# Attention with a threshold, then SoLU and a layer norm, in one kernel: the copy of o ahead of V on ScalarE, the last tokens' product mixed in later, loads of q, k and v in other rounds, and the last tile's h a tile sooner

## The chip, the cores and the metric

The kernel runs on one core of a Trainium2 chip. The metric is the device time of one execution in microseconds (us). Names used here: TensorE (PE in the profile, its weight loads PEld), VectorE (DVE), ScalarE (ACT), GpSimd (POOL), and SyncE (SP), whose queue issues nearly all DMAs. Each of these takes its own instructions in the order in which the program lists them.

## The reference

Eight batches of eight heads, 576 tokens, 64 numbers a head; then 4608 tokens of width 512 through a layer of width 1024 and back, all in float32.

```python
scores = (1/sqrt(64)) * q @ k.T
scores = where(scores >= max(scores) - tau, scores, -1e9)
attn   = exp(scores - max) / (sum + 1e-9)
x      = heads side by side of attn @ v            # 4608 x 512
h      = x @ w_in                                  # 4608 x 1024
solu   = h * softmax(h)
ln     = (solu - mean) / sqrt(var + 1e-6) * g_ln
out    = ln @ w_out                                # 4608 x 512
```

## The kernel before

The program is laid out in rounds, by hand (`manual_schedule`): the loop at the end of the kernel counts `rnd` and lists, for each engine, what this round adds. There are 144 rounds with scores (NS), 18 to a batch (PER), and then a tail without scores. A batch starts at round 18 b, so batches of even number start at a round that divides by 4, and those of odd number at one that leaves 2.

**Attention.** Each round makes the scores of one slot (`scores`, L479): two heads, 128 rows of queries, 576 keys. VectorE takes the row limit (`maxes`, L501), ScalarE makes the threshold and the exponential (`ramp` L516, `exps` L525), GpSimd divides by the sum a round later (`normalise`, L535), VectorE turns the weights in blocks into T (`blocks`, L547), and after each second slot the SP queue moves T into wT (L556, L558; L563 for the last tokens). About three rounds later the product with v runs on TensorE (`attend_steps`, L589), for which `take("pv")` needs a free pair of PSUM banks, and ScalarE copies the result to xh or xe (`attended`, L621). A slot's kind is 0 or 1 for the first 512 tokens and 2 for the last 64 of all heads ("the last tokens"). A product of kind 2 is woven into half an h tile: its 72 matmuls come 24 at a time after the second, third and fourth of h's four steps (L661).

**The second part.** It works on tiles of 128 tokens. The two halves of h come in two rounds (`ff_h`, L654, in the tail L644), the two halves of o in two further rounds (`ff_o`, L759), so that in the steady state four rounds make one tile: h, h, o of the tile before, o. Between h and o of a tile lie the following steps, listed in the rounds after the second half of h, which is in round r:

- r: maximum of h (VectorE, `ff_max` L669), exponential u (ScalarE, `ff_exp` L678)
- r+1: u times h (VectorE, `ff_mul` L684), which frees h's PSUM pair; the sum's inverse (GpSimd)
- r+2: mean and variance (VectorE L699, L700; GpSimd L703 to L710, the last being nb), then V, the normalised tile (ScalarE, `ff_norm` L720), at the end of the round
- r+3: u normalised in place (VectorE, `ff_norm2` L725), four DMAs that swap groups of 32 rows from u into V (`ff_swap`, L736: V<-u)
- r+4: the turned tile uT (VectorE, `ff_turn` L746), which o needs

The copy of a finished o (ScalarE, `ff_out` L774; L771 and L772 for the last one) stands at the start of the round after o's second half, and frees o's PSUM pair. Its store (L794) comes at the end of that round. V has one buffer.

Four lists say what a round does besides: `begin` at its start, `middle` after the scores' steps, `late` near its end, and `load_at` after that. There are four PSUM pairs: two (s0, s1) for the scores, two (p0, p1) for h, o and the products; in the tail all four are free for h, o and products.

**Loads.** From batch 2 on, q and k come as whole rows (`load_natural`, L195), are scaled (q, on GpSimd, L199), turned on VectorE (L213, "flip") and moved into qT and kT by DMAs (L215). v comes in four parts of 576, 288, 144 and 144 KB per half batch (`load_v`, L160). Tags q and k have two buffers, v three. The tables `load_at` and `turn_at` say in which round each is listed. A load of q or k is listed three rounds ahead of its turn. The first two batches load in another way, which the change leaves alone.

**The tail.** After round 143, h and o of the last tiles alternate; a new h is started while fewer than three tiles lie `between` h and o. The very last tile (tokens xe) holds the last tokens of batches 6 and 7.

Of the kernel before, what the change touches and what calls it, by code (L numbers as in the profile page):

```python
# [20 lines left out]
def kernel(  # L21
# [81 lines left out]
    def take(name):  # L103
        tag = pairs_free.pop(0)
        return tag, ps_mm.tile([P, 1024], F32, tag=tag, name=name)


    def fence(first):
        m = nc.gpsimd.memset(mark, 0.0)
        for mm in first:  # L110
            sync(m, mm)
        return m

    def sync(late, first):
        tc.add_manual_dep(
            late.ins, first.ins.name,
            mybir.DependencyInfo(mybir.DependencyClass.Sync, mybir.DependencyReason.DATA),
            reason="rows change banks",
        )
# [72 lines left out]
    def load_natural(i, nm, a):  # L192
        raw = loads.tile([P, 4, 4, D], F32, tag=nm, name=nm)
        natural[i, nm, a] = raw = raw.rearrange("p h t d -> p (h t d)")[:, 0 : NK * D]
        nc.sync.dma_start(out=raw, in_=qk_rows[nm][a, 64 * i : 64 * i + P])  # L195
# [429 lines left out]
    def tokens(t):  # L625

        if len(t) == 1:
            return xe[t[0]]
        b, kind, m = t
        return xh[b, kind][:, :, P * m : P * m + P]  # L630


    def ff_h(t, part, split, beside=()):
        beside = iter(beside)
        x = tokens(t)
        if part == 0:
            tag, h = take("h_ps")
            ffn[t] = dict(h=h, tag=tag, split=split)
        d = ffn[t]
        h = d["h"]  # L640
        if not d["split"]:
            f = slice(512 * part, 512 * part + 512)
            for c in range(NP):
                nc.tensor.matmul(  # L644
                    out=h[:, f], lhsT=x[:, c], rhs=w1_parts[:, c, part],
                    start=c == 0, stop=c == NP - 1,
                )
            return
        last = []
        for c in range(NP):  # L650
            for r in range(2):
                f = slice(512 * (part ^ r), 512 * (part ^ r) + 512)
                for y in range(2):
                    mm = nc.tensor.matmul(  # L654
                        out=h[ROWS[y], f], lhsT=x[ROWS[r], c, ROWS[y]], rhs=w1_parts[ROWS[r], c, part ^ r],
                        start=part == 0 and c == 0, stop=part == 1 and c == NP - 1,
                    )
                    if part and not last:
                        sync(mm, d["fence"])
                    last.append(mm)  # L660
            for _, _ in zip(range(24 * (c > 0)), beside):  # L661
                pass
        if part == 0:
            d["fence"] = fence(last[-4:])

    def ff_max(t):
        d = ffn[t]
        d["nm"] = small.tile([P, 1], F32, tag="hm", name="hm")
        nc.vector.tensor_reduce(out=d["nm"], in_=d["h"], axis=AX.X, op=ALU.max, negate=True)  # L669

    def ff_exp(t):
        d = ffn[t]

        starts.append(t)
        tag = "xh1" if rnd > NS and len(starts) % 2 else "u"
        d["u"] = work.tile([P, DFF], F32, tag=tag, bufs=1, name="u")
        d["se"] = small.tile([P, 1], F32, tag="se", name="se")
        nc.scalar.activation(  # L678
            out=d["u"], in_=d["h"], func=AF.Exp, bias=d["nm"], scale=1.0, accum_out=d["se"]
        )  # L680

    def ff_mul(t):
        d = ffn[t]
        nc.vector.tensor_tensor(out=d["u"], in0=d["h"], in1=d["u"], op=ALU.mult)  # L684
        pairs_free.append(d["tag"])
# [29 lines left out]
    def ff_norm(t):  # L715
        d = ffn[t]
        rs, nb = d["norm"]
        d["V"] = V = work.tile([P, 2, DFF // 2], F32, tag="V", bufs=1, name="V")
        u = d["u"].rearrange("p (g n) -> p g n", g=2)
        nc.scalar.activation(out=V, in_=u, func=AF.Identity, bias=nb, scale=rs)  # L720
# [79 lines left out]
    NS = len(slots)  # L800
# [13 lines left out]
    for i in range(NP, 2 * NP):  # L814
        at = (13, 15, 19, 20)[i - NP]
# [7 lines left out]
    load_at = {}  # L823
# [12 lines left out]
    for i in range(2 * NP, NPAIR, 2):  # L836
        b, hf = divmod(i // 2, 2)
        ats = ((-5, -3), (-1, 1)) if hf else ((-13, -11), (-9, -7))
        if b == 2:
            ats = ((-3, -2), (-1, 1)) if hf else ((-13, -11), (-9, -5))  # L840
        for nm, pieces_at in zip("qk", ats):
            for a, at in enumerate(pieces_at):
                at += PER * b
                load_at.setdefault(at - 3, []).append(
                    lambda i=i, nm=nm, a=a: load_natural(i, nm, a)
                )
                turn_at[at] = i, nm, a
                if nm == "q":
                    scale_at[at - 1] = i, a
        for j in range(2):  # L850
            ends_at[PER * b + ats[0][1] + 4 + j] = i + j
        for part, at in enumerate((4, 5, 5, 7) if hf else (-9, -7, -5, -3)):
            load_at.setdefault(PER * b + at, []).append(
                lambda b=b, hf=hf, part=part: load_v(b, hf, (part,))
            )

    with tc.manual_schedule():
# [20 lines left out]
        ready = []  # L878
        rnd = 0
        prev = cur = None  # L880

        between, starts, turns = [], [], []
        quarter = 0
        w2_done = False

        begin, middle, late = {}, {}, {}
        while True:
            more = rnd < NS
            if not more and not (
# [3 lines left out]
                break  # L893
            for job in begin.pop(rnd, []):
                job()
            if rnd == NS:
                pairs_free += ["s0", "s1"]
                if prev is not None:
                    between.append(prev)
                    prev = None  # L900
                if quarter == 2:
                    between.append(cur)
                    cur = None
                    quarter = 0
                assert quarter != 3
            if (
                cur is None and quarter == 0 and ready and ready[0][0] <= rnd
                and (more or len(between) < 3)
            ):
                cur = ready[0][1].pop(0)  # L910
                if not ready[0][1]:
                    ready.pop(0)
# [4 lines left out]
            if more:  # L917
# [3 lines left out]
                while preps and preps[0][0] <= rnd and preps[0][1] <= room:  # L921
                    _, n, make, _ = preps.pop(0)
# [47 lines left out]
            beside = ()  # L970
            if attending is not None and attending[1] == 2 and step is not None:
                beside = attend_steps(attending)
            if step == ("h", 0):
                ff_h(cur, 0, rnd + 1 < NS, beside)
                quarter = 1
            elif step == ("h", 1):
                ff_h(cur, 1, None, beside)
                quarter = 2
                late.setdefault(rnd, []).append(lambda t=cur: (ff_max(t), ff_exp(t)))
                late.setdefault(rnd + 1, []).append(lambda t=cur: (ff_mul(t), ff_sum(t)))  # L980
                middle.setdefault(rnd + 2, []).append(lambda t=cur: ff_stats(t))
                late.setdefault(rnd + 2, []).append(lambda t=cur: ff_norm(t))
                middle.setdefault(rnd + 3, []).append(lambda t=cur: (ff_norm2(t), ff_swap(t)))

                at = rnd + 4 if more or not ready else rnd + 6
                if cur == (0, 1, 1):
                    middle.setdefault(rnd + 6, []).append(lambda t=cur, at=rnd + 6: ff_turn(t, at))
                else:
                    late.setdefault(at, []).append(lambda t=cur, at=at: ff_turn(t, at))
                if not more:  # L990
                    between.append(cur)
                    cur = None
                    quarter = 0
            elif step == ("o", 0):
                if prev is not None:
                    ff_o(prev, 0)
                quarter = 3
            elif step == ("o", 1):
                if prev is not None:
                    ff_o(prev, 1)  # L1000
                    last = not (more or ready or cur or between)
                    begin.setdefault(rnd + 1, []).append(lambda t=prev, last=last: ff_out(t, last))
                    late.setdefault(rnd + 1, []).append(lambda t=prev, last=last: ff_store(t, last))
                prev, cur = cur, None
                quarter = 0
            if attending is not None:
# [3 lines left out]
                b, kind, hp = attending  # L1010
# [62 lines left out]
```

## Time and profile before

| | us |
|---|---|
| median of three runs (lowest, highest) | 874.81 (871.08, 876.6) |
| the profiled execution | 876.26 |
| its span, first to last instruction | 874.4 |
| idle time of VectorE before the limits, waiting for scores (L501 for L479) | 56.0 |
| idle time of ScalarE before V, waiting for nb (L720 for L710) | 54.8 |
| idle time of VectorE before uT, waiting for the swap (L746 for V<-u) | 37.5 |
| idle time of VectorE before u, waiting for V (L725 for L720) | 22.2 |

"Busy" is the time in which an engine works on an instruction; DMA-issuing instructions of SP do not count as busy. A releaser after an arrow is the work whose end let the waiting instruction start. The ends of matmuls in the profile are modelled and overlap with the next ones, so differences between starts are safer than durations on TensorE. In the list of waits, the numbers are the sum in us, the number of times and the longest. The median time from issue to landing is 6.5 us for a wT transfer of 288 KB, 3.7 us for one of the four swaps of 64 KB, 6.4 us for a v part of 576 KB and 5.9 and 5.7 us for a q and a k load of 288 KB. A mean of 193 GB/s is moved over the span.

### The profile page before, as it was taken

The page shows a single profiled execution, that of the slowest core. Times are in us where ns is not written, and L with a number is a line of the kernel's source. Part 1 is how long each engine was busy: PE and PEld are TensorE (multiplying, and loading weights), DVE is VectorE, ACT ScalarE, POOL GpSimd, SP SyncE. Part 2 cuts the span into 40 slices and gives each one's busy share as a digit, 9 for nine tenths or more (in the row PEclk, how much of TensorE's full clock was granted, in tenths as well). Part 3 has the DMA queues.
Part 4 walks back from the last instruction along what each step waited for, and adds up shares of the span by engine and source line. Part 5 has one row for each costly group of instructions (what it writes and reads, how often), then busy time and mean ns, then how long its engine had stood idle before and what let it go on. Part 6 is the DMA issues. An engine that isn't in the chain of part 4 may idle for free. (4 is left out here: it accounts for less than half of the span.)

```text
span 874.4 us, 36148 instructions
## 1 busy us (share of the span) xinstructions
PE 822.0 (94%) x15361; PEld 599.8 (69%) x15361; DVE 682.6 (78%) x1248; ACT 573.1 (66%) x1153; POOL 499.4 (57%) x938
## 2 busy tenths in 40 slices
PE   5667999999999999999999999999899999999997
PEld 3455676775688887767677767777666667777555
DVE  5998787888788887888788887888778887787351
ACT  5877776776767666767666766666666666675121
POOL 2887656556556656565656655665565665555120
PEclk9879899999999999999999999999999999999999
DMA  7999968798788887897888886888688876655222
GB/s 231 261 273 246 219 160 214 202 237 212 194 218 223 205 189 186 199 243 175 199 211 216 213 195 173 216 228 207 158 219 223 212 187 165 162 141 138 64 49 49
DMA packets 83712, 168.54 MB, mean 193 GB/s; under 512 B 15448, under 2 KB 45152, under 8 KB 83552
## 3 DMA queue, kind: packets, MB, share of 16 engines
q1 hardware_dynamic: 82416, 164.25, 75.9%
q8 instruction: 120, 1.97, 1.0%
q10 hardware_dynamic: 1136, 2.00, 0.7%
q14 instruction: 40, 0.33, 0.1%
HBM read 46.14 MB, written 9.44 MB: 64 GB/s over the span
## 5 line engine op out<-in xcount | busy, mean ns | idle before, releaser
L759 PE MATMUL o_ps<-w,uT 64*64 64x256 f32 x4608 | 269.2, 376 | 5.1 <-DVE uT L746 3.1
L759 PEld LDWEIGHTS o_ps<-w,uT 64*64 64x64 f32 x4608 | 214.8, 133 | 68.5 <-issue 17.1
L516 ACT ACTIVATE w<-s_ps,nth 128x576 f32<-128x576 f32 x280 | 196.7, 740 | 92.4 <-DVE nth L501 84.8
L501 DVE CUSTOM_DVE_ANT_0 w<-s_ps,tau_t 128x576 f32<-128x576 f32 x280 | 199.5, 748 | 64.1 <-PE s_ps L479 56.0
L535 POOL TENSOR_SCALAR w<-w,sm 128x576 f32<-128x576 f32 x288 | 221.3, 780 | 14.3
L547 DVE STREAM_TRANSPOSE T<-w 128x576 f32<-128x576 f32 x288 | 207.7, 755 | 23.7 <-POOL w L535 21.1
L654 PE MATMUL h_ps<-w,xh 64*64 64x512 f32 x1856 | 222.5, 592 | 0.0
L525 ACT ACTIVATE w<-w,ntau 128x576 f32<-128x576 f32 x288 | 219.9, 770 | 0.0
L589 PEld LDWEIGHTS pv<-wT,v 64*64 64x64 f32 x5760 | 173.6, 136 | 50.1 <-issue 28.1
L589 PE MATMUL pv<-wT,v 64*64 64x128 f32 (+1 forms) x5760 | 176.3, 264 | 13.0 <-DMA wT<-T 5.3
L479 PE MATMUL s_ps<-kT,qT 64*64 64x64 f32 (+1 forms) x2048 | 173.5, 419 | 13.1 <-ACT w L516 11.8
L654 PEld LDWEIGHTS h_ps<-w,xh 64*64 64x64 f32 x1856 | 111.3, 134 | 82.7 <-issue 59.3
L532 POOL TENSOR_SCALAR sm<-sm 128x2 f32<-128x2 f32 x144 | 37.4, 259 | 171.6 <-ACT w L525 167.6
L533 POOL TENSOR_TENSOR sm<-sm,mone 128x2 f32<-128x2 f32 x144 | 108.1, 751 | 12.0
L479 PEld LDWEIGHTS s_ps<-kT,qT 64*64 64x64 f32 x2048 | 70.2, 139 | 21.9 <-ACT w L516 17.5
L720 ACT ACTIVATE V<-u,nb,rs 128x1024 f32<-128x1024 f32 x36 | 44.7, 1241 | 54.8 <-POOL nb L710 54.8
L746 DVE STREAM_TRANSPOSE uT<-V 128x1024 f32<-128x1024 f32 x36 | 44.4, 1234 | 37.5 <-DMA V<-u 37.5
L621 ACT COPY xh<-pv 128x256 f32<-128x256 f32 x64 | 24.9, 389 | 63.7 <-PE pv L589 63.7
L678 ACT ACTIVATE u<-h_ps,hm 128x1024 f32<-128x1024 f32 x36 | 40.2, 1115 | 31.4 <-DVE hm L669 21.7
L525 ACT ACTIVATION_READ_ACCUMULATOR w<-w,ntau 128x1 f32 x288 | 56.2, 195 | 0.0
L725 DVE TENSOR_SCALAR u<-u,rs,nb 128x1024 f32<-128x1024 f32 x36 | 36.5, 1014 | 22.2 <-ACT V L720 22.2
L684 DVE TENSOR_TENSOR u<-h_ps,u 128x1024 f32<-128x1024 f32 x36 | 42.8, 1189 | 10.9 <-ACT u L678 10.9
(90 smaller groups left out, 573.0 us busy)
## 6 DMA issues: line engine op xcount, KB each, us to landing
wT<-T SPq DMA_DIRECT2D x160, 288.0 KB, 6.5
wT<-T SPq DMA_DIRECT2D x64, 576.0 KB, 5.5
V<-u SPq DMA_DIRECT2D x144, 64.0 KB, 3.7
out_dram<-ob SPq DMA_DIRECT2D x71, 128.0 KB, 2.8
q<-in_q_dram SPq DMA_DIRECT2D x24, 288.0 KB, 5.9
qT<-flip SPq DMA_DIRECT2D x48, 144.0 KB, 3.2
k<-in_k_dram SPq DMA_DIRECT2D x24, 288.0 KB, 5.7
kT<-flip SPq DMA_DIRECT2D x48, 144.0 KB, 3.6
```

Source lines behind the costliest of these rows:

```text
L479: nc.tensor.matmul(out=ps[h][ROWS[y], ks], lhsT=lhsT, rhs=d["kT"][ROWS[h], ks], start=True, stop=True,)
L501: nc.vector.tensor_tensor_reduce(out=w, in0=ps[:, 0:S], in1=(zero if loose else tau_t).to_broadcast([P, S]), scale=1.0, scalar=BIG, op0=AL ...
L516: nc.scalar.activation(out=d["w"][x], in_=d["w"][x] if d["loose"] else d["ps"][x][:, 0:S], func=AF.Prelu, bias=d["nth"][x], scale=-1.0, al ...
L525: nc.scalar.activation(out=w, in_=w, func=AF.Exp, bias=ntau, scale=1.0, accum_out=sm[:, x : x + 1])
L533: nc.gpsimd.tensor_tensor(out=sm, in0=sm, in1=mone, op=ALU.pow)
L535: nc.gpsimd.tensor_scalar(out=w, in0=w, scalar1=sm[:, x : x + 1], scalar2=1.0, op0=ALU.mult, op1=ALU.mult)
L547: nc.vector.transpose(out=T[:, :, r, h, :], in_=w)
L589: nc.tensor.matmul(out=to, lhsT=d["v"][ROWS[u], (h0 + h - u) % 4 if b > 1 else h0 + h, m ^ 4 * u if m < 8 and b < 2 else m,], rhs=rhs, sta ...
L654: mm = nc.tensor.matmul(out=h[ROWS[y], f], lhsT=x[ROWS[r], c, ROWS[y]], rhs=w1_parts[ROWS[r], c, part ^ r], start=part == 0 and c == 0, st ...
L720: nc.scalar.activation(out=V, in_=u, func=AF.Identity, bias=nb, scale=rs)
L746: nc.vector.transpose(out=uT, in_=d["V"].rearrange("p y (m x) -> p m y x", x=32))
L759: nc.tensor.matmul(out=d["o"][ROWS[z], 512 * (r ^ other) : 512 * (r ^ other) + 256], lhsT=d["uT"][ROWS[r], m].rearrange("p y x -> p (y x)" ...
```

## The change

1. V (`ff_norm`) is listed at the start of round r+3, after the jobs of `begin`, and no longer at the end of round r+2. As the copy of o is such a job, it now stands ahead of V. Tiles whose h ends in the last rounds before the tail keep the old place.
2. Where the product of the last tokens is woven into the second half of an h tile, its matmuls come 36 at a time after the third and the fourth step. In the first half of a tile it stays as it was.
3. A load of q or k from batch 3 on is listed in the next round at or before its old one that divides by 4. The parts of v are listed in rounds that depend on whether the batch's number is odd; relative to the batch's start these are 2, 5, 5, 6 (odd) and 3, 4, 4, 7 (even) for the second half of the heads, where it was 4, 5, 5, 7, and -11, -7, -3, -3 (odd) and -9, -5, -1, -1 (even) for the first, where it was -9, -7, -5, -3. For batch 2 the first half's rounds are as before.
4. In the tail, the last tile (a single one in its group) may start h when three tiles already lie between h and o; and the tile before it turns uT in round r+4 and not r+6. By the order of instructions, TensorE then runs h, h, and four o tiles behind each other, where it ran h, o, h and three o tiles.

```diff
-            for _, _ in zip(range(24 * (c > 0)), beside):
+            for _, _ in zip(range(36 * (c > 1) if part else 24 * (c > 0)), beside):
...
-                load_at.setdefault(at - 3, []).append(
+                load_at.setdefault(at - 3 if b == 2 else (at - 3) // 4 * 4, []).append(
                     lambda i=i, nm=nm, a=a: load_natural(i, nm, a)
                 )
...
-        for part, at in enumerate((4, 5, 5, 7) if hf else (-9, -7, -5, -3)):
+        if hf:
+            v_ats = (2, 5, 5, 6) if b % 2 else (3, 4, 4, 7)
+        elif b == 2:
+            v_ats = -9, -7, -5, -3
+        else:
+            v_ats = (-11, -7, -3, -3) if b % 2 else (-9, -5, -1, -1)
+        for part, at in enumerate(v_ats):
             load_at.setdefault(PER * b + at, []).append(
...
             for job in begin.pop(rnd, []):
                 job()
+            if rnd in norms:
+                ff_norm(norms.pop(rnd))
...
-                and (more or len(between) < 3)
+                and (more or len(between) < 3 + (len(ready[0][1][0]) == 1))
...
-                late.setdefault(rnd + 2, []).append(lambda t=cur: ff_norm(t))
+                if rnd + 6 < NS:
+                    norms[rnd + 3] = cur
+                else:
+                    late.setdefault(rnd + 2, []).append(lambda t=cur: ff_norm(t))
                 middle.setdefault(rnd + 3, []).append(lambda t=cur: (ff_norm2(t), ff_swap(t)))
-                at = rnd + 4 if more or not ready else rnd + 6
+                at = rnd + 4 if more or not ready or len(ready[0][1][0]) == 1 else rnd + 6
```

More of the change, by code (lines that the diff above doesn't have):

```diff
@@ L884 @@
         w2_done = False
-        begin, middle, late = {}, {}, {}
+        begin, middle, late, norms = {}, {}, {}, {}
         while True:
```

## The prediction

> **What bounds the kernel now.** I read the page's busy shares and slices first, then who waits for whom on TensorE, then the time lines of single rounds.
>
> ```profile
> PE 822.0 (94%) x15361; PEld 599.8 (69%) x15361; DVE 682.6 (78%) x1248; ACT 573.1 (66%) x1153; POOL 499.4 (57%) x938
> PE   5667999999999999999999999999899999999997
> PEclk9879899999999999999999999999999999999999
> ```
>
> TensorE is the bound from about 110 us on: every slice is at 9 tenths at full clock. Before that, VectorE is full (21.8 of 22 us between 44 and 66 us) and the weights are being unpacked. A busy share does not say how much is left to take, so I differenced the starts of TensorE's groups in its time line. A round of scores takes 0.97 us, half an h tile 3.43, half an o tile 3.45, one attention product 1.97. A round is then 4.43 us (scores and o) or 6.37 us (scores, h, product), and most rounds after round 36 (209 us) have these lengths to 0.01 us. What rounds last beyond this sums to 22.6 us from round 19 to round 142, 13.4 us of it after round 36. That, the tail and the first 110 us are all that any reordering can win. The table of TensorE's waits from 200 us to the end names the causes:
>
> ```profile
> PE pv L589 <- ACT ob L774: 3.6, 3, 1.6
> PE o_ps L759 <- DVE uT L746: 3.1, 4, 1.0
> PE pv L589 <- DMA wT<-T: 1.8, 3, 0.6
> PE pv L589 <- issue: 1.5, 1, 1.5
> PE pv L589 <- ACT xh L621: 1.0, 1, 1.0
> ```
>
> The columns are the sum, the number of times, the longest. Three waits are for the copy of o, four for the turned uT (three in the loop, one in the tail), three for the turned weights wT. The change has one part for each, so I follow each in the time line.
>
> **The change part by part.** *V and the copy of o on ScalarE (rounds 34, 75, 111).* ScalarE's time line before one such wait, and TensorE's:
>
> ```profile
> 422.18 1.24 ACT L720 ACTIVATE V<-u,nb,rs 128x1024 f32<-128x1024 f32 x1 [1.18 <-POOL nb L710]
> 423.32 0.56 ACT L774 COPY ob<-o_ps 128x512 f32<-128x512 f32 x1
> ```
> ```profile
> 423.94 0.97 PE L589 MATMUL pv<-wT,v 64*64 64x64 f32 x46 [0.80 <-ACT ob L774]
> ```
>
> V stands ahead of the copy and waits 1.18 us for GpSimd's nb; the copy frees the PSUM pair that the product needs. TensorE ended that o tile about 420.4 us and ScalarE was free at 421.0. In the new order the copy fits into V's own wait: 421.0 to 421.5, and V still starts at 422.18. The product would start when its half tile of h lets it, at 421.16 + 1.72 = 422.9. So all three waits go: 1.55 + 0.80 + 1.22 = 3.6 us. In round 34 V waited 3.92 us for nb, so the room is larger there. The same swap happens for nearly all of the 36 tiles; elsewhere ScalarE gets 0.5 us of slack that TensorE does not use. The price: if o ended late, V, the update of u and the V<-u transfers would slip by up to the copy's 0.56 us. In each round I looked at, o ended before ScalarE was free, so I take 0. Once, at 92 us, V falls behind a unit of weights (em, L290), which waits for VectorE until 92.6 us: V ends near 94.5 instead of 93.1, and VectorE started the update of u only at 94.66. Hidden; 1.4 us if not. The wait for xh in round 39 (1.0 us) stays: there ScalarE's next step waited for VectorE's limits, not for V.
>
> *The last tokens' product one step of h later (rounds 56, 92, 128).* TensorE:
>
> ```profile
> 316.85 2.15 PE L654 MATMUL h_ps<-w,xh 64*64 64x512 f32 x16
> 318.56 0.28 PE L589 MATMUL pv<-wT,v 64*64 64x64 f32 x4
> 319.64 0.86 PE L589 MATMUL pv<-wT,v 64*64 64x64 f32 x42 [0.64 <-DMA wT<-T]
> ```
>
> The product is reached after two of h's four steps, at 318.56, and its first matmuls wait until the fourth wT transfer lands at 319.50 (issued 313.48). In the new order three steps run first, 3 x 0.86 us: it is reached at 319.42. The three rounds last 0.77, 0.98 and 0.58 us too long; I leave a rest of 0.2 and 0.4 in the first two and take 0.57 + 0.58 + 0.58 = 1.7 us. The instruction order shows this regrouping in four rounds; in the fourth, in batch 1, no wait is seen and I take 0. The matmuls are the same, so nothing is added; if wT came 0.9 us later than now, the old wait would be back.
>
> *Loads of q, k, v in other rounds.* The SP queue before the wait of 0.71 us for uT at 346.96 us:
>
> ```profile
> 333.89 2.92 SPq L558 DMA_DIRECT2D wT<-T  x2
> 336.86 0.98 SPq L160 DMA_DIRECT2D v<-in_v_dram  x1
> 337.94 0.95 SPq L195 DMA_DIRECT2D q<-in_q_dram  x1
> 338.99 2.48 SPq L736 DMA_DIRECT2D V<-u  x4
> ```
>
> VectorE had u ready at 336.08. The swap V<-u is issued 2.91 us later, behind a 576 KB load of v and a 288 KB load of q, lands last at 345.45 (6.46 us after its first issue), and VectorE turns uT from 345.57, having waited 2.95 us. Over the 36 tiles, this lag from u to issue is 1.5 to 3.0 us where a load stands in front and 0.4 to 0.5 us where none does. The swap is issued in rounds with number 3 modulo 4; before, q and k loads come in even rounds, half of them just before the swap. From batch 3 on they all go to rounds 0 modulo 4, and v goes to the ends of rounds 3 and 0, behind the swap. Swaps go out about 2 us earlier. The rounds that are too long for this cause are 61, 97, 133 (1.01, 1.20, 0.94) and, with no gap shown, 69, 101, 109 (0.43, 0.23, 0.30): 4.1 us, all of which I book. The Trainium skill speaks against this ("DMA: Bandwidth & Descriptors", section "Issuing engines are not separate DMA queues"): all issuing engines share the same 16 DMA engines, and the sequencer's time for an issue is usually small beside the transfer. By that rule the same bytes through the same engines gain nothing and this part is 0. In this trace one issue takes SP 0.6 to 1.1 us, and the swap's wait in the queue alone (2.91 us) is larger than the stall; I go by the row.
>
> The moved loads have a price. Two loads now follow each other (2 x 0.95 us of SP), then flips (about 1.3 us) and the next round's wT. The queue's sum per four rounds stays about 7 us of wT, 2.5 to 3.3 of swap, 1.4 of stores, 2.6 of flips, 3.5 of loads: 17 to 18 of 21.6 us. Loads now come at least as early as before, with the turn of the old buffer at least three rounds back, so I see no new wait of SP for a buffer. v's first part waits for the previous batch's last product in the same round, which TensorE ends before VectorE reaches the next round; the wT behind it needs that VectorE work anyway. I take 0 here and keep 3 us as the bound above.
>
> *The last tile's h a tile sooner.* TensorE at the end:
>
> ```profile
> 840.38 7.13 PE L644 MATMUL h_ps<-w,xe 128*128 128x512 f32 x16
> 847.44 14.04 PE L759 MATMUL o_ps<-w,uT 64*64 64x256 f32 x256
> 862.46 7.14 PE L759 MATMUL o_ps<-w,uT 64*64 64x256 f32 x128 [0.97 <-DVE uT L746]
> ```
>
> Before, from h's end (847.5) to uT (862.3) the last tile has 14.8 us of small steps, and only 14 us of o beside it. Now h runs at 833.3 to 840.4, and three o tiles, 21 us, cover the steps. Its row maximum changes places with the previous tile's update of u on VectorE. Walking the steps with their rows: V of the last tile waits for uT of the tile before (V has one buffer), near 850; V 1.24, u 0.81, swap and landing 3.9, uT 1.25 end at about 857.3; TensorE comes for it at 861.6. The copies of o wait on ScalarE behind this V until 851; four PSUM pairs still suffice. Gain 0.97 us, taken as 0.9.
>
> *Sum:* 3.6 + 1.7 + 4.1 + 0.9 = 10.3 us. The waits named "issue" (1.56 us at 137.9, 1.53 at 628, about 1 at 240) have no cause in the program and may land elsewhere: -3 to +2. For small new waits I take 1 us back, which gives 9.3. The profiled execution took 876.26 us (span 874.4 and 1.8 around it), 1.45 above the median of the runs, 874.81. So 867.0 on its own scale, 865.5 against the median; I say **866**.
>
> **The rivals.** *The waits are refilled.* A TensorE that comes 0.6 to 3 us sooner meets the next late thing, xh or wT. For: at least 5 of the 22.6 us of overlength are waits for things that no part touches. Against: ScalarE, VectorE and SP have 15 to 30% spare in this stage, and most rounds have no overlength at all. If half the gain is refilled: 4 to 6 us, 869 to 871. *The transfers are bound, not the queue:* the rule above; then loads count 0 and the rest gives 6.2, less 1: about 869.5; it falls in the same case. *It doesn't do what it says:* if o ended after ScalarE was free, the swap on ScalarE would be void; the times above exclude that. With nothing gained, 874 to 876.
> *Slower: bunched transfers delay wT.* In rounds 3 modulo 4 v parts go out ahead of the wT of the next round, now in eight places with a 576 KB part among them (batches 2 to 7 have twelve). Before, such a wT was issued from 346.29, landed at 355.88 and was wanted by TensorE at 359.28: a margin of 3.4 us, from which on each further us costs TensorE one. The swap behind 864 KB took 6.46 us; if wT were held up by as much, 3.1 x 8 = 25 us would be lost, less the 5.2 us that the other parts leave: 894. It decides from a delay of 4.1 us on. Against: 576 KB is about 3 us at the 200 GB/s that the page shows, and the swap ahead of it leaves 2 us sooner.
>
> **How the numbers follow.** All parts work (gain 7.5 to 13): 67%, 862 to 868. Half refilled or loads void: 23%, 868.5 to 872. Nothing: 5%. Slower by wT: 5%. The bound of 1% is about what a measurement can tell here, since three runs spread over 0.6%; 1% below 874.81 is 866.1, in the middle of the likeliest case, so faster gets three quarters of its 67%: 0.50; the rest of it, the refilled case and the case of nothing give same 0.45; slower 0.05. The range 861 to 873 leaves out the slow case, most of the empty one and a little at the fast end.
>
> **What would show it.** Right: the copy of o starts before V and the PE's waits for it are gone; V<-u is issued within 0.6 us of u in nearly every tile; rounds 61, 97, 133 last 4.43 us; rounds 56, 92, 128 wait under 0.4 us for wT; no wait of 0.97 before the last o. Wrong: new TensorE waits for wT in rounds 3 modulo 4, V later than nb, or a changed first 110 us, which my sum holds fixed.

## The result, and the profile after

| | before | after |
|---|---|---|
| median (lowest, highest), measured beside each other, us | 874.35 (871.08, 876.6) | 865.54 (858.89, 867.81) |
| runs | 6 | 6 |
| profiled execution, us | 876.26 | 866.93 |
| its span, us | 874.4 | 865.1 |

The ratio after to before is 0.9894, with a 95% interval of 0.9853 to 0.9934: about 9 us, or 1.1%, faster. One execution of the first experiment below, 876.54 us and 1.5% above that kernel's fastest, is left out of its figures. The page of the changed kernel shows the same amount of work in less time:

```profile
PE 820.7 (95%) x15361; PEld 626.8 (72%) x15361; DVE 682.1 (79%) x1248; ACT 574.1 (66%) x1153; POOL 497.0 (57%) x938
PE   5667899999999999999999999999999999999997
```

The matmuls are the same in number, and the busy time of matmuls, VectorE, ScalarE and GpSimd has moved by less than 3 us. That of the weight loads (PEld), which overlap the matmuls, differs by 27 us, but it lies anywhere between 579 and 627 us in the ten profiles of this case. The slices are at 9 tenths from the sixth to the last but one; before, they were so from the fifth, but for one slice at 8 that the prediction passed over. What went is waiting, which the list of TensorE's waits between 192 us and the end shows (who waits, for what: sum in us, number, longest):

```profile
PE pv L589 <- ACT xh L621: 1.0, 1, 1.0
PE o_ps L759 <- issue: 0.9, 1, 0.9
PE s_ps L479 <- ACT w L516: 0.5, 2, 0.3
PE pv L589 <- DMA wT<-T: 0.3, 1, 0.3
PE s_ps L479 <- issue: 0.3, 1, 0.3
```

No row is left for ob (the copy of o) or for uT, and wT is down to one wait of 0.3 us. The wait for xh, which no part touches, is still there, as the prediction said.

Differences between the starts of TensorE's groups give each round's length; those of the rounds that moved, in us:

| rounds | before | after | part |
|---|---|---|---|
| 34, 35 | 8.25, 6.37 | 6.80, 7.31 | copy of o, but these rounds vary by themselves |
| 75 | 7.63 | 6.51 | copy of o |
| 111 | 9.86 | 6.59 | copy of o, and an "issue" wait of 1.53 |
| 56, 92, 128 | 7.53, 7.74, 7.33 | 6.73, 7.02, 6.51 | product later |
| 61, 97, 133 | 5.43, 5.62, 5.36 | 4.43, 4.45, 4.43 | loads |
| 69, 101, 109 | 4.85, 4.65, 4.72 | 4.43, 4.43, 4.43 | loads |
| 40 | 6.68 | 7.21 | none |
| 41, 76, 93 | 5.08, 6.39, 4.43 | 5.65, 7.00, 4.89 | none, waits named "issue" |
| 143 to the start of the last matmul | 71.89 | 70.38 | tail |

From round 36 to round 142 the rows with a part give 3.27 + 1.12 + 2.34 + 4.03 = 10.76 us, the two rows without a part take 2.17 back, and 8.59 remain; summed over all rounds of this stretch it is 8.55. The tail gives 1.51, rounds 34 and 35 together 0.51, rounds 19 to 33 0.34. The first 19 rounds took 1.89 longer. Together that is 9.0 of the 9.3 us between the spans.

Of the 2.17 us that were taken back, 1.64 stand in rounds 41, 76 and 93, in waits that the profile names "issue" because no semaphore is missing. The weight load at which TensorE stops in round 76, and a line of the list of DMA queues (packets, MB, share of the DMA engines):

```profile
428.15 0.20 PEld L654 LDWEIGHTS h_ps<-w,xh 64*64 64x64 f32 x7 [0.81 <-issue]
q8 instruction: 120, 1.97, 1.0%
```

The traces tell what is missing. Count all of TensorE's instructions in order (matmuls, weight loads and its semaphore instructions). In the ten profiles of this case there are 24 waits of this name of more than 0.5 us on weight loads in rounds 41, 66, 76, 93 and 111. Each of them falls on an instruction whose number leaves 193 or 194 when divided by 256 (15,042 in round 76 and 18,625 in round 93 of this profile), and each ends 1.2 to 1.6 us after a packet of queue 8 has landed; a moment taken at random would do so in 6% of cases. Queue 8 brings 120 packets of 16 KB, and TensorE has 30,894 instructions: one packet for some 257 of them. So in these waits TensorE stands at the end of one block of its own instructions and waits for the next. Why these blocks come late and others do not is not shown.

The mechanism of each part can be read in a few lines. ScalarE's time line around an o tile (start, duration, work, and in brackets the idle time before it and who ended it):

```profile
420.32 0.57 ACT L774 COPY ob<-o_ps 128x512 f32<-128x512 f32 x1
421.59 1.24 ACT L720 ACTIVATE V<-u,nb,rs 128x1024 f32<-128x1024 f32 x1 [0.70 <-POOL nb L710]
```

The copy now stands ahead of V, in the time that V has to wait for GpSimd's nb anyway: 0.70 us of that wait are still left over. TensorE in round 56:

```profile
318.70 3.00 PE L654 MATMUL h_ps<-w,xh 64*64 64x512 f32 x24
321.27 1.48 PE L589 MATMUL pv<-wT,v 64*64 64x64 f32 x70
```

24 matmuls (three steps of h) run before the product, and no bracket stands behind it: wT is there. And SP's queue in round 59:

```profile
334.96 3.05 SPq L558 DMA_DIRECT2D wT<-T  x2
338.11 3.00 SPq L736 DMA_DIRECT2D V<-u  x4
341.15 1.62 SPq L794 DMA_DIRECT2D out_dram<-ob  x2
```

Nothing stands between wT and the swap. Before, v and q did. The tail:

```profile
825.46 7.03 PE L644 MATMUL h_ps<-w,xe 128*128 128x512 f32 x16
832.42 27.86 PE L759 MATMUL o_ps<-w,uT 64*64 64x256 f32 x512
```

Four o tiles run as one group of 512 matmuls without a wait. Among VectorE's and ScalarE's own waits over the whole span two have shrunk much, from 54.8 and 37.5 us:

```profile
ACT V L720 <- POOL nb L710: 35.1, 33, 5.0
DVE uT L746 <- DMA V<-u: 16.3, 16, 4.6
```

The first shrank by 0.6 us for each of its 33 waits, because a copy of 0.57 us fills part of it. The second says that swaps now land earlier relative to VectorE's turn. By itself it does not say whether that is because they leave sooner or travel faster; three of the experiments ask that.

### The profile page after: what moved, and what is told of

Read it like the earlier page. It is cut to its first block, busy times and chain, and to the rows that moved or that the text cites. A ratio compares the mean times of both kernels' runs of the same rounds, so it can differ in the third digit from the quotient of the medians.

```text
span 865.1 us, 36118 instructions
## 1 busy us (share of the span) xinstructions
PE 820.7 (95%) x15361; PEld 626.8 (72%) x15361; DVE 682.1 (79%) x1248; ACT 574.1 (66%) x1153; POOL 497.0 (57%) x938
## 4 chain that ended last, share of the span: by engine, by line
PE 82%; DMA 6%; ACT 4%; DVE 3%; issue 2%; POOL 2%; SPq 1%; ACTq 0%; DVEq 0%; POOLq 0%
PE o_ps L759 26%; PE h_ps L654 22%; PE s_ps L479 15%; PE pv L589 14%; PE h_ps L644 3%; DMA wT<-T 2%; ACT w L516 1%; DVE w L501 1%; DMA raw<-in_moe_w_out_dram 1%; ACT w L525 1%; DMA q<-in_q_dram 1%; DMA raw<-in_moe_w_in_dram 1%; DVE T L547 1%; PE s_ps L344 1%; POOL w L535 1%
## 5 line engine op out<-in xcount | busy, mean ns | idle before, releaser
L759 PE MATMUL o_ps<-w,uT 64*64 64x256 f32 x4608 | 272.3, 376 | 2.6 <-issue 2.6
L759 PEld LDWEIGHTS o_ps<-w,uT 64*64 64x64 f32 x4608 | 222.8, 133 | 55.3 <-ACT xh L621 10.9
L535 POOL TENSOR_SCALAR w<-w,sm 128x576 f32<-128x576 f32 x288 | 220.7, 778 | 14.3
L589 PEld LDWEIGHTS pv<-wT,v 64*64 64x64 f32 x5760 | 175.9, 135 | 38.5 <-issue 18.5
L479 PE MATMUL s_ps<-kT,qT 64*64 64x64 f32 (+1 forms) x2048 | 180.9, 422 | 14.0 <-ACT w L516 12.4
L654 PEld LDWEIGHTS h_ps<-w,xh 64*64 64x64 f32 x1856 | 124.1, 133 | 72.5 <-issue 31.6
L479 PEld LDWEIGHTS s_ps<-kT,qT 64*64 64x64 f32 x2048 | 75.2, 139 | 23.3 <-ACT w L516 18.4
L746 DVE STREAM_TRANSPOSE uT<-V 128x1024 f32<-128x1024 f32 x36 | 44.3, 1230 | 16.6 <-DMA V<-u 16.3
L669 DVE TENSOR_REDUCE hm<-h_ps 128x1 f32<-128x1024 f32 x36 | 42.9, 1192 | 5.9 <-PE h_ps L654 3.1
```

Source lines behind the costliest of these rows:

```text
L479: nc.tensor.matmul(out=ps[h][ROWS[y], ks], lhsT=lhsT, rhs=d["kT"][ROWS[h], ks], start=True, stop=True,)
L535: nc.gpsimd.tensor_scalar(out=w, in0=w, scalar1=sm[:, x : x + 1], scalar2=1.0, op0=ALU.mult, op1=ALU.mult)
L589: nc.tensor.matmul(out=to, lhsT=d["v"][ROWS[u], (h0 + h - u) % 4 if b > 1 else h0 + h, m ^ 4 * u if m < 8 and b < 2 else m,], rhs=rhs, sta ...
L654: mm = nc.tensor.matmul(out=h[ROWS[y], f], lhsT=x[ROWS[r], c, ROWS[y]], rhs=w1_parts[ROWS[r], c, part ^ r], start=part == 0 and c == 0, st ...
L746: nc.vector.transpose(out=uT, in_=d["V"].rearrange("p y (m x) -> p m y x", x=32))
L759: nc.tensor.matmul(out=d["o"][ROWS[z], 512 * (r ^ other) : 512 * (r ^ other) + 256], lhsT=d["uT"][ROWS[r], m].rearrange("p y x -> p (y x)" ...
```

## The experiments

Each kernel ran beside the kernel before on the same chip. The first four share one set of runs of it, with a median of 877.09 us, and the last four another, with 876.15; beside the change itself it gave 874.35. Times of different sets are therefore compared by their ratio to before. The kernel with the old tail runs the program of the change up to round 143, so what differs between these two profiles up to there is not due to an edit. "Over" means what a stretch of rounds lasts beyond the sum of the round lengths that the prediction worked with, in the profiled execution.

**One part undone at a time.** V ahead of the copy again:

```diff
-                if rnd + 6 < NS:
-                    norms[rnd + 3] = cur
-                else:
-                    late.setdefault(rnd + 2, []).append(lambda t=cur: ff_norm(t))
+                late.setdefault(rnd + 2, []).append(lambda t=cur: ff_norm(t))
```

> The changed kernel with V back at the end of round r+2, ahead of the copy of o; all else as changed. My theory: TensorE's waits for the copy of o come back in rounds 75 and 111 (about 0.8 and 1.2 us, round lengths 7.4 to 7.8 us where they are 6.5 now); in rounds 34 and 35 together almost nothing changes (14.1 us now, 14.6 before), since V's own wait for nb holds ScalarE there in either order. Sum about +2.5 us, 866 to 870. Rival (the copy's place is worth nothing, the later mixing or the earlier swap covers those rounds): no wait for the copy, rounds 75 and 111 stay at 6.5 us.

Measured: 864.39 us (863.51 to 866.99), 0.9874 (0.9825 to 0.9922) of before. TensorE's waits:

```profile
PE pv L589 <- ACT ob L774: 2.4, 3, 0.9
PE pv L589 <- issue: 1.5, 1, 1.5
```

The three waits for ob are back: 0.94, 0.67 and 0.75 us, in rounds 34, 75 and 111. So is the "issue" wait in round 111, which lasts 9.50. But the time is that of the full change. Over rounds 36 to 142 this execution is 5.79 us over, against 4.82 after and 5.70 with the old tail, whose program is the same there as after: rounds 40 and 41 (6.38, 4.43) and 76 (6.38) are without the stalls that the changed kernel's own profile shows. In round 76 that is no accident. It lasts 6.38 to 6.40 us in the three kernels with V first (before, this one, and the one with the loads alone) and 6.94 to 7.77 in the seven with the copy first, each time with the wait for a block of instructions. Rounds 75 and 76 together last 13.9 to 14.0 us with V first and 13.4 to 14.3 with the copy first. So what the copy gains in round 75 is mostly waited for one round later. The waits for ob are shown; that they are worth anything in the time is not.

The product mixed in as before:

```diff
-            for _, _ in zip(range(36 * (c > 1) if part else 24 * (c > 0)), beside):
+            for _, _ in zip(range(24 * (c > 0)), beside):
```

> The changed kernel with the last tokens' product mixed in 24 at a time after the second step of h, in both halves. My theory: waits for wT come back in rounds 56, 92 and 128, which then last 7.3 to 7.7 us where they last 6.7, 7.0 and 6.5 now; about +2.3 us. Rival (the moved loads already bring wT sooner): those rounds last under 6.8 us.

Measured: 864.76 us (861.27 to 871.04), 0.9878 (0.9845 to 0.9912).

```profile
PE pv L589 <- DMA wT<-T: 1.6, 4, 0.7
PE pv L589 <- issue: 1.2, 1, 1.2
```

Waits for wT rise from 0.3 to 1.6 us, and rounds 56, 92, 128 last 7.24, 7.80 and 7.01: 1.8 us more than after, at the places foretold. Two microseconds are 0.2% of the time, and the medians do not show them.

The loads where they were:

```diff
-                load_at.setdefault(at - 3 if b == 2 else (at - 3) // 4 * 4, []).append(
+                load_at.setdefault(at - 3, []).append(
...
-        for part, at in enumerate(v_ats):
+        for part, at in enumerate((4, 5, 5, 7) if hf else (-9, -7, -5, -3)):
```

> The changed kernel with the loads of q, k and v in their old rounds. My theory: the swap V<-u is again issued 1.5 to 3 us after u is ready, and rounds 61, 97 and 133 last 5.4 us and rounds 69, 101, 109 4.65 to 4.85 us where all six last 4.43 now; about +4 us. Rival (the copy of o ahead of V takes the load off those rounds, and the loads are worth nothing): the six rounds stay at 4.43 us.

Measured: 870.54 us (864.68 to 873.52), 0.993 (0.9898 to 0.9963), where the change has 0.9894 (0.9853 to 0.9934): about 3 us more, with intervals that overlap. Of the four kernels that lack one part it is the slowest; the other three, beside the same runs of before, have 0.9874, 0.9878 and 0.9901. TensorE's first wait, and SP's queue in round 59:

```profile
PE o_ps L759 <- DVE uT L746: 3.8, 4, 1.4
```
```profile
331.22 2.98 SPq L558 DMA_DIRECT2D wT<-T  x2
334.24 1.48 SPq L160 DMA_DIRECT2D v<-in_v_dram  x1
335.82 0.60 SPq L195 DMA_DIRECT2D q<-in_q_dram  x1
336.53 3.05 SPq L736 DMA_DIRECT2D V<-u  x4
```

v and q again stand between wT and the swap, 2.3 us of issue time; the swap leaves 3.13 us after u is ready (0.98 after the change). Rounds 61, 97, 133 last 6.08, 6.12 and 5.72, more than foretold; rounds 69, 101, 109 last 4.43, 4.58 and 4.60, less than foretold. Together the six are 4.9 us longer than after.

The tail as it was:

```diff
-                and (more or len(between) < 3 + (len(ready[0][1][0]) == 1))
+                and (more or len(between) < 3)
...
-                at = rnd + 4 if more or not ready or len(ready[0][1][0]) == 1 else rnd + 6
+                at = rnd + 4 if more or not ready else rnd + 6
```

> The changed kernel with the old tail: h of the last tile after the o of another tile, and the old round for the turn. My theory: TensorE waits about 1 us for uT before its last o again, and the time from the start of round 143 to the end grows by 1 to 1.5 us. Rival (the tail is hidden by the earlier o copies): no wait, under 0.3 us.

Measured: 867.82 us (862.82 to 870.33), 0.9901 (0.9863 to 0.994). The wait before the last o tile is back, and round 143 lasts 72.12 instead of 70.38:

```profile
853.74 7.14 PE L759 MATMUL o_ps<-w,uT 64*64 64x256 f32 x128 [1.00 <-DVE uT L746]
```

So the tail is worth 1.7 us, of which the wait is 1.00. Some 0.4 us more lie in the spacing: here the five tiles before the last o (h, o, h, o, o) take 35.24 us without the wait, from 817.50 on, and in the new order the same number (h, h, o, o, o) takes 34.8. The remaining 0.3 I did not place. The ratio, 0.9901 against 0.9894, could not show it.

**Queue or transfers?** The prediction took the gain of the loads from SP's queue, against the skill's rule. The rival: loads and swaps share the transfer engines, and what counts is when bytes move. First, the q and k loads in the rounds 2 modulo 4, just ahead of the swap's turn in SP's queue, with everything else as after:

```diff
-                load_at.setdefault(at - 3 if b == 2 else (at - 3) // 4 * 4, []).append(
+                load_at.setdefault(at - 3 if b == 2 else (at - 5) // 4 * 4 + 2, []).append(
```

> The changed kernel with q and k loads of batches 3 to 7 in rounds 2 modulo 4, just ahead of the swap, as bunched as in the change (v as in the change). My theory (what counts is what stands ahead of the swap in SP's queue): the lag from u to the first V<-u rises to about 2 us and more in nearly every tile, uT comes 2 to 3 us later, and TensorE waits for uT in many of the rounds 1 modulo 4, 0.2 to 1.4 us each: 4 to 15 us more than the changed kernel, 869 to 880. Rival (bunching itself, or fewer rounds with loads, brings the gain): same as the changed kernel, no wait for uT.

Measured: 877.62 us (875.48 to 881.17), 1.0018 (0.9992 to 1.0044) of before. The whole gain of all four parts is gone because the loads of q and k stand in the wrong place.

```profile
PE o_ps L759 <- DVE uT L746: 5.7, 9, 1.0
PE pv L589 <- DMA wT<-T: 2.3, 3, 1.0
```

Nine waits for uT; the swap is now issued 2.15 us after u on average. Rounds 85, 113, 117, 121, 53 and others last 5.4 to 5.7 instead of 4.43; rounds 36 to 142 are 18.95 us over. Since bytes have moved in time as well as in the queue, this does not yet exclude the rival.

The loads alone, on the kernel before (the two load edits of the change and nothing else):

> The kernel before with the change of the load rounds alone. My theory: 4 us less than before, rounds 61, 97 and 133 at 4.43 us, while the waits for the copy of o (rounds 34, 75, 111), for wT (56, 92, 128) and before the last o stay. Rival (the four parts need each other: a TensorE that runs ahead meets the next wait): under 2 us less, waits for uT elsewhere.

Measured: 871.9 us (868.08 to 876.33), 0.9962 (0.9936 to 0.9988), 4.3 us less than before.

```profile
PE pv L589 <- ACT ob L774: 1.5, 2, 0.8
PE pv L589 <- issue: 1.5, 1, 1.5
PE pv L589 <- DMA wT<-T: 1.4, 3, 0.6
PE o_ps L759 <- DVE uT L746: 1.0, 1, 1.0
```

What this part does not touch is still waited for: ob, wT, and uT once, before the last o. The three waits for uT in the loop are gone. Of the ob waits only two remain, since round 34 is free (6.42, before 8.25). The edit can't be the cause: the first load that it moves is listed in round 36, and up to there both kernels run the same program. In round 33 GpSimd waited 3.30 us for a load of q here and 5.17 before, so that nb came sooner. The wait in round 34 thus comes and goes from one execution to the next.

Then the other queue. The loads keep their old rounds (as in the third kernel above), but those of rounds 2 modulo 4 are issued from ScalarE's queue. The same bytes go to the same places, and the loads are listed in the same rounds; what differs is the queue they stand in, and with it the moment at which they leave:

```diff
+            queue = nc.scalar if rnd % 4 == 2 else nc.sync
-            nc.sync.dma_start(
+            queue.dma_start(
```

> The changed kernel with the old load rounds, where those loads that are listed in rounds 2 modulo 4 are issued from ScalarE's queue and not SP's. Same bytes, same rounds. My theory (SP's queue ahead of the swap): V<-u is issued within 0.5 us of u again, the swap lands 1.5 to 3 us sooner than with the loads ahead of it on SP, and the waits for uT in rounds 61, 97, 133 are gone, about -4 us against e3_loads_old less what ScalarE loses to 0.6 to 1 us an issue. Rival (the 16 DMA engines are shared, the bytes alone delay the swap): the issue comes sooner but the last landing doesn't, and the waits for uT of 1.0 to 1.4 us stay.

Measured: 866.11 us (861.85 to 866.61), 0.988 (0.9835 to 0.9925), as after. Beside the same runs of before, that is 11.5 us less than with the loads of q and k just ahead of the swap. ScalarE's queue and SP's in round 59 (lines of the code shift by one or two):

```profile
329.81 0.39 ACTq L161 DMA_DIRECT2D v<-in_v_dram  x1
330.24 0.51 ACTq L197 DMA_DIRECT2D q<-in_q_dram  x1
```
```profile
332.38 3.77 SPq L560 DMA_DIRECT2D wT<-T  x2
336.25 3.98 SPq L738 DMA_DIRECT2D V<-u  x4
```

v and q leave from the other queue, and the swap follows wT at once. It still leaves 1.69 us after u here, since wT's own two issues took 3.77 us; the expected 0.5 us held in 13 of the 25 tiles below. TensorE no longer waits for uT:

```profile
PE pv L591 <- ACT xh L623: 1.0, 1, 1.0
PE o_ps L761 <- issue: 0.4, 1, 0.4
```

The means are over tiles 7 to 31 (the first tile is 0), the sums over the whole span, in us:

| kernel | u ready to first issue of the swap (mean) | issue to last landing (mean) | VectorE's waits for the swap before uT (sum) | rounds of the q and k loads |
|---|---|---|---|---|
| before | 1.60 | 5.69 | 37.5 | even |
| loads in their old rounds | 1.61 | 5.66 | 45.3 | even |
| just ahead of the swap | 2.15 | 5.72 | 64.8 | 2 modulo 4 |
| loads alone moved | 0.61 | 5.76 | 14.3 | 0 modulo 4 |
| after | 0.68 | 5.57 | 16.3 | 0 modulo 4 |
| old rounds, ScalarE's queue | 0.73 | 5.72 | 23.2 | even, half on ScalarE |

The third column holds to 0.2 us; the second moves by 1.5. The last kernel alone would not exclude the rival: counted from the start of round 59, v and q leave some 6 us sooner on ScalarE's queue than on SP's, and in 22 of the 25 tiles no load was under way when the swap left. The kernel before settles it. There 17 of the 25 swaps left while a load of q, k or v was under way, and took 5.62 us on average; the other eight took 5.85. After, none met a load, and they took 5.57. Transfers as the bound would have made the 17 slower. (On ScalarE's queue three swaps did meet a load, and took 7.01 us; three are too few to say whether that is its doing.) What the change took away is the wait in SP's queue: before, 1.96 us from u to the swap where a load was issued between them, 0.46 where none was.

**A step further with the product.** In both halves of an h tile, 36 matmuls of it after the third and the fourth step:

```diff
-            for _, _ in zip(range(36 * (c > 1) if part else 24 * (c > 0)), beside):
+            for _, _ in zip(range(36 * (c > 1)), beside):
```

> The changed kernel with the last tokens' product mixed in 36 at a time after h's third step in the first half of a tile too. My theory: the wait of 1.0 us for xh in round 39 shrinks to 0.1 (one step of h is 0.86 us), rounds 75 and 111 stay as they are, -0.9 us in all, which the times can't tell. Rival: the wait moves to the end of the round, nothing gained.

Measured: 867.89 us (864.82 to 869.2), 0.9902 (0.9867 to 0.9938). The wait for xh goes and round 39 lasts 7.07 instead of 7.91, but round 40 lasts 8.57 instead of 7.21, and this row appears:

```profile
PE pv L589 <- DMA wT<-T: 1.8, 3, 1.0
```

One wait was exchanged for another, of wT. This is refilling at one place; the time says nothing either way. None of the eight is distinguishably faster than the change itself.

## Why the prediction was right, step by step

The forecast was 866 us, against 865.54 measured, and the likeliest case held: all parts work. It is exact beyond its merit, since terms off in both directions cancelled.

- **The loads.** Booked 4.1 us in six rounds; these gave 4.03. Made alone, they bring 4.3 us in the time, with an interval (0.9936 to 0.9988) that excludes equal times; undone, they cost about 3, with intervals that overlap. Here the step that decided was to set aside the rule of the Trainium skill ("DMA: Bandwidth & Descriptors", section "Issuing engines are not separate DMA queues") that the sequencer's time for an issue is usually small beside the transfer. Taken issue by issue it holds here too: 0.6 to 1.5 us, beside 5.6 to 5.8 from the swap's first issue to its last landing. But issues add up in one queue: for four transfers of 64 KB behind two larger loads they cost 2 to 3 us, while the time from issue to landing stayed. One sign did not come out as written: V<-u left within 0.6 us of u in 18 of the 36 tiles, not in nearly every one, and after 1.5 at most.
- **The copy of o.** Booked 1.22 and 0.80 in rounds 111 and 75: 3.27 and 1.12 came. In round 111, 1.53 of this is an "issue" wait, which the prediction had said may land elsewhere; with V first it stood there in three profiles of three, and with the copy first it was absent in five of seven. Without it 1.74 remain. A part of the misfit is one of measure: for the copy the prediction booked the gap in the list of waits, for the loads the overlength of the round, and the gap is the smaller. Round 34 lost 1.88 us for a gap of 1.55, and round 75 lost 1.12 for 0.80. And the gain of round 75 did not stay, as the first experiment shows. The one place where the prediction feared a late V, the first tile, showed it: V started 1.63 us after nb, and VectorE waited 0.20 us for it.
- **Round 34.** The copy's largest term was mis-sized: 1.55 booked, 0.51 came from rounds 34 and 35 together. In round 35 of the after profile the scores waited for ScalarE, which stood behind V's own 3.9 us wait for nb. With V first these two rounds were 1.88, 1.27 and 0.05 us over, with the copy first 1.37 and 1.03, and five times nothing. It depends on when nb comes, and one profile of it is no basis for a term. The expectation for the first experiment repeated that mistake: it had these rounds unchanged, and a wait for ob of 0.94 came up in round 34.
- **The product.** Booked 1.7: measured 0.80 + 0.72 + 0.82 = 2.3. What was mis-sized is the length of these rounds without a wait: the overlengths of the prediction (7.53 less 0.77, for one) make it 6.76 us, and round 128 now lasts 6.51. Above that, rests of 0.2 and 0.5 us stand in rounds 56 and 92, about as foreseen. Undoing the part brings 1.8 back in these rounds.
- **The tail.** Booked 0.9, measured 1.5 here and 1.7 against the experiment. The term held the wait only and not the wider spacing where h and o alternate. The margin was smaller than worked out: the last uT ended 1.7 us before TensorE came, not 4.3, since the last V, which waits for uT of the tile before, started about 1.5 us later than I had walked it, the last swap took 0.7 longer, and TensorE itself came some 0.4 sooner.
- **What was taken back.** 1 us booked, and 2.17 found in rounds 40, 41, 76 and 93. Rounds 40 and 41 vary by themselves: with the old tail, the same program there, they last 6.64 and 4.43. Round 76 is long wherever the copy stands first, and round 93 is longer than 4.43 in all kernels but before, each time at the start of a block of instructions. The three "issue" waits that the prediction listed without a cause (at 137.9, 240 and 628 us) fall on such places too.
- **The first 110 us**, held fixed, took 1.89 longer up to round 18. The program order up to round 14 is the same in all the kernels, and in the ten profiles these 19 rounds take from 106.7 to 111.2 us. It is spread and not an effect of the change, but the spread of 4.5 us is as large as any of the four parts. Some of it is the same wait: 0.59 us in round 16 before, 1.29 after, and 3.17 with the loads on ScalarE's queue.
- **The rivals.** Refilled: 2.2 of some 10.8 us, far from half; but in round 75 it is what happened, and what TensorE met there was neither xh nor wT but its own instructions. Transfers bound: against it stands the swap's travel time, the same with loads under way as without. Slower by bunched loads delaying wT: no wait for wT in a round 3 modulo 4 appears; the only one left is 0.3 us, in round 40. (By the tables of rounds there are nine places with such a part ahead of wT, not eight.)

Still open: whether the copy of o and the product bring anything that the time can show. Their waits go and come with them in the profiles, but each is worth about 0.2% and the intervals are 0.6 to 1%. Open too is what makes a block of instructions late.

## What to carry to other kernels

When a small transfer lies on the path, look at what stands ahead of it in the queue that issues it and measure from the end of its producer to its first issue, apart from issue to landing. Moving large loads behind it, or to another engine's queue, costs no bytes; here it was the only one of the four parts whose worth the time shows. And take a stall from several profiles before putting it in a sum: with V first, the wait for ob was 0.67 to 0.80 us in round 75, but anything from nothing to 1.55 in round 34, which hangs on when a load lands. Then read the round after the one that is mended as well: a stall may only have moved there.

## What the runs showed of the hardware that was not expected

An issue's time is not fixed. In round 59 v and q took SP 1.48 and 0.60 us, and ScalarE's queue 0.39 and 0.51; the swap's four issues took 3.00 us after, and 3.98 with the loads on ScalarE's queue. One round is too little for a rule.

TensorE can wait for its own instructions. The "issue" waits above 0.5 us in rounds 41, 66, 76, 93 and 111 all stand at the same place in a block of 256 of its instructions, 1.2 to 1.6 us after an instruction packet has landed. They last 0.6 to 1.8 us and fall on these few blocks of the 120; in round 76 it depended on whether the wait for ob had held TensorE up in the round before, for the others what decides it was not shown. They make one profile's list of stalls differ from the next by 1 to 3 us.

The start, where weights are loaded and unpacked, differs by 4.5 us between profiles of kernels that run the same program there up to round 14: about as much as the largest part moved.
